# A fused attention and GEGLU block on one core: the head's loads and warm-ups, three weight tiles, and a new plan for every engine

## The chip, the cores and the metric

The kernel runs on one core of one Trainium2 chip. The time is the device time of one launch in microseconds. A core has TensorE (PE in the profile: matmuls, transposes, and its separate weight loads, PEld), VectorE (DVE), ScalarE (ACT), GpSimd (POOL) and SyncE (SP, which here only issues DMAs). They run side by side and wait for each other on semaphores. TensorE's clock is granted by a throttle; the profile shows the granted share.

Three runs of the kernel before gave 257.41, 257.42 and 258.76 us; the median is 257.42.

## The reference

One transformer block with conditioning, x being [2048, 512] in bf16:

```
mod = silu(c) @ w_mod            # six vectors of 512: sa, ca, ga, sb, cb, gb
h = layernorm(x) * (1 + ca) + sa
q, k, v = split(h @ wqkv)        # 32 heads of 16
logits[s, w] = q[s] . k[s - 2*w] / 4,  w = 0..7;  masked where s - 2*w < 0
o = softmax_w(logits) @ v[s - 2*w]
x = x + ga * (o @ wo)
h = layernorm(x) * (1 + cb) + sb
x = x + gb * ((gelu(h @ w_gate) * (h @ w_up)) @ w_down)   # inner width 1792
```

## The kernel before

**Slabs.** The 2048 rows go in four slabs of 512 (`sg` 0 to 3). Per slab: first layer norm (`norm`, VectorE statistics st and mv, rstd on GpSimd, normalised xn on VectorE), transposes to hTp in PSUM on TensorE, and their copy to hT with scale and shift (`transp_ev`, usually on ACT). Then 12 QKV groups of four 128x512 matmuls (L499), each copied out by ACT to qT, kT or vT. v goes through DRAM (`vscr`) and comes back as V4, shifted for the eight window places. VectorE multiplies q with shifted k (pq, L548, eight of 128x2048 per slab), and TensorE sums each head with 32-column matmuls (LTp, L562). ACT copies the logits to LT; they are transposed (LNp), and VectorE and ACT do the softmax (mx, LT, e, ssum, rinv). The probabilities are transposed back (PTp, PT), VectorE multiplies them with V4 (pv, L664, eight per slab), TensorE sums (o_ps, L676) and applies wo (x_ps, L696), VectorE adds x (L705). The second norm follows in the same way (LN2). The feed-forward part has 14 pairs of groups g_ps and u_ps (L724), ACT's gelu and copy (gl, ub), VectorE's product hht, and 56 matmuls y_ps with Wd (L736), an add on VectorE (ot) and a store.

**Modulation.** The six vectors are matmuls of silu(c) with blocks of w_mod (wm0 to wm5). wm1 and wm0 are wanted first (modT_ps, L324, 32 small matmuls, then ACT's copies to modT and scl, which the first hT needs), wm3 and wm4 for the second norm, wm2 and wm5 as rows (mb_ps, L338; copied to gB) by which wo and Wd are scaled on VectorE (woP L388, WdP L382).

**Tiles and queues.** wqkv is one tile of 128 x 4 x 1536, filled by three loads (one for q, one for k, one for v); the weights of a QKV group are strided columns of it. WdP takes over its buffer after the last QKV matmul. The SP queue issues, in this order: four tiles of x for slab 0, wm1, wm0, wqkv 0 and 1, x of slab 1, wqkv 2, x of slabs 2 and 3, wm2, four pieces of wo, wm3, wm4; later wm5, V4, Wg, Wu, WdP and the stores. ACT's queue only loads c. PSUM has four buffers for large results (mm), two each for the attention (att) and the transposes (tp).

**The order on each engine** is made by a small planner in the kernel's own text (`Planner`). Every stage is a generator of steps (`Op`: engine, assumed duration, what it needs, the buffers it takes and gives). At each point the planner looks for the step that can begin first, allows others on the same engine within a slack, and takes the one with the lowest due value from the table `PR` (per stage and slab). The chosen order is then fixed: each engine runs its instructions in it and only waits for semaphores. So a changed assumed duration, slack or due value reorders all engines.

**The head.** While the first loads run, TensorE runs matmuls on a zeroed tile (`warmup`, 13 at the start, and three more after modT among the transposes) so that its clock is granted. In slab 0 the four hT pieces are 512 wide, two on ACT and two on VectorE.

Of the kernel before, what the change touches and what calls it, by code (L numbers as in the profile page):

```python
# [17 lines left out]
PR = {  # L18
    "ga": 10.2, "mb": 13.7, "gb": 46.9, "wds": 31.7, "wos": 3.3, "ln1": [33, 7.6, 53.2, 33.6], "t1": [7.7,
    8.8, 0.2, 36.7], "h1": [27.6, -4.6, 27.3, 18], "qkv": [55.7, 70, 3.1, 73.3], "qev": [70, 3.6, 50, -5.6],  # L20
    "v": [23, 3, 28, 42.1], "pq": [37.5, 68.8, 111.2, 118.6], "lmm": [0, -3.1, 28.6, 13], "lev": [-13.2,
    -11.4, -3.6, 23], "smm": [7.6, 1, 66.9, 56.1], "soft": [49.9, 29.5, -6.6, 41.2], "e": [60, 20.5, -1.9,
    5.6], "ptp": [-1.9, 37.5, 19.8, 2.5], "pt": [-7.8, 1.3, 60.8, 29.5], "pv": [-4.8, 27.7, 27, 77.3], "pvmm":
    [-3.9, -0.4, 5, 23.9], "pvev": [2.3, 34.7, 76.2, -4.9], "x1mm": [-4.5, 28.3, 3, 16.2], "x1": [8, 0, 40,
    3], "ln2": [21, -5.2, -2, 3], "t2": [24.9, 1.2, -1.7, 28], "h2": [-21.4, 15.2, 3.9, 73.9], "ffn": [78.2,
    36.9, 67.9, 132.2], "act": [20.9, 46.5, -1.1, 30.2], "hh": [8, 25.1, 77.1, 8], "st": [8.2, 85, 3.8, 28.2],
# [25 lines left out]
class Planner:  # L52
# [5 lines left out]
    def __init__(self):  # L58
        self.clock = {e: 0.0 for e in self.LAT}
        self.threads = []  # L60
        self.done = {}
        self.slack = {"PE": 0.31, "ACT": 13.31, "DVE": 0, "POOL": 0, "SP": 0}
        self.far = {"PE": 0, "ACT": 0.03, "DVE": 0.2, "POOL": 0, "SP": 0}
        self.table = None
        self.quad = False
        self.dma = 0.0
        self.log = []
# [19 lines left out]
    def run(self):  # L87
# [5 lines left out]
        while live:  # L93
# [18 lines left out]
            if eng == "PE":  # L112
                if self.quad and not op.quad:
                    w += 0.1
                self.quad = op.quad
# [23 lines left out]
def kernel(  # L139
# [26 lines left out]
    def pool(name, bufs, **kw):  # L166
# [5 lines left out]
          "wm": 1, "hh": 16, "o": 2, "wA": 1, "mm": 4, "att": 2, "tp": 2}  # L172
# [28 lines left out]
    wqkv = pools["wA"].tile([P, DT, 3 * D], BF16, name="wqkv", tag="wA")  # L201
# [39 lines left out]
    def warmup(n, zero):  # L241
        if zero:
            yield Op("DVE", 0.25, lambda: nc.vector.memset(gB[:], 0.0), fire="warm")
        for k in range(n):
            def f(k=k):
                if k == 0:
                    B["warm"] = T("mm", [P, SG], F32, "warm_ps")
                nc.tensor.matmul(B["warm"][:], lhsT=gB[:, 0:P], rhs=gB[:], start=True, stop=True)
            yield Op("PE", 0.43, f, after=["warm"] if zero else ["warm", "mp0"], take=[SL["mm"]] if k == 0 else [],
                     give=[SL["mm"]] if k == n - 1 else [])  # L250
# [3 lines left out]
    def loads():  # L254
# [3 lines left out]
        def ldx(sg, c0=0, c1=CPS):  # L258
            def f():
                if c0 == 0:  # L260
                    B["x", sg] = T("x", [P, CPS, D], BF16, "x")
                nc.sync.dma_start(out=B["x", sg][:, c0:c1, :],  # L262
# [3 lines left out]
        def ldwm(b):  # L266
            def f():
                B["wm", b] = T(WM[b], [P, 4, D], BF16, "wm")
                nc.sync.dma_start(
# [11 lines left out]
        def ldq(b):  # L281
            return ld(wqkv[:, :, b * D:(b + 1) * D], wq_v[:, :, b * D:(b + 1) * D])

        def ldwd():
            B["WdP"] = T("wA", [P, FT, D], BF16, "WdP")
            nc.sync.dma_start(out=B["WdP"][:], in_=B_w_down.rearrange("(ft p) d -> p ft d", p=P))
# [5 lines left out]
        def act_q():  # L292
            yield Op("ACT", 0.55, ldc, fire="c", lat=0.05, dma=True)

        def sp_q():
            for k in range(CPS):
                yield Op("SP", 0.5, ldx(0, k, k + 1), fire=f"x0.{k}", lat=mb(0.125))
            yield Op("SP", 0.55, ldwm(1), take=[SL[WM[1]]], fire="wm1", lat=mb(0.5))
            yield Op("SP", 0.55, ldwm(0), take=[SL[WM[0]]], fire="wm0", lat=mb(0.5))
# [14 lines left out]
            yield Op("SP", 0.65, ldwd, fire="Wd", lat=mb(1.8), take=[SL["wA"]], after=[f"qkv.{g}.l" for g in range(NSG)])  # L314
# [31 lines left out]
    def mods():  # L346
# [4 lines left out]
        def f1():  # L351
            B["scp"] = T("tp", [P, 2, SG], BF16, "scp")
            nc.tensor.transpose(B["scp"][:, 0, 0:4], s4[:], ident[0:4, 0:4])
        yield Op("PE", 0.2, f1, after=["s4", "ident"], take=[SL["tp"]], fire="scp")

        def f2():
            nc.scalar.copy(out=scT[:], in_=B["scp"][:, 0, 0:4])
        yield Op("ACT", 0.2, f2, after=["scp"], give=[SL["tp"]], fire="scT")

        yield Op("PE", 0.6, cols(1, 1, "mp0"), after=["wm1", "scT"], take=[SL["mm"]], give=[SL["h2"]])  # L360
        yield Op("PE", 0.6, cols(0, 0, "mp0"), after=["wm0"], give=[SL["h2"]], fire="mp0")
# [7 lines left out]
    def mods_b():  # L369
        yield Op("PE", 0.6, cols(3, 0, "mp1"), after=["wm3", "scT", "wm4"], take=[SL["mm"]], give=[SL["h2"]])  # L370
        yield Op("PE", 0.6, cols(4, 1, "mp1"), after=["wm4"], give=[SL["h2"]], fire="mp1")
# [7 lines left out]
    def wdscale():  # L379
        for h in range(7):  # L380
            def wds(h=h):
                nc.vector.tensor_tensor(out=B["WdP"][:, 2 * h:2 * h + 2, :], in0=B["WdP"][:, 2 * h:2 * h + 2, :],  # L382
                                        in1=_ap(gB[:], [[0, 2], [1, D]]), op=ALU.mult)
            yield Op("DVE", 0.63, wds, after=["gb", "Wd"], fire=f"WdS{h}")
# [11 lines left out]
    def norm(key, src, ready, ev, parts=((0, 4),)):  # L396
# [8 lines left out]
        for c4 in range(CPS):  # L405
# [5 lines left out]
            yield Op("DVE", 0.80, f, after=ready(c4), fire=f"{ev}.st{c4}")  # L411
            for a, b in parts:
                if c4 == b - 1:
                    def f(a=a, b=b):
                        nc.vector.tensor_scalar_add(out=st_k["rstd"][:, a:b], in0=st_k["mv"][:, a:b, 1], scalar1=1e-5)  # L415
                    yield Op("DVE", 0.15, f, fire=f"{ev}.ve{a}")
# [4 lines left out]
                    yield Op("POOL", 1.1, f, after=[f"{ev}.ve{a}"], fire=f"{ev}.rs{a}")  # L421
# [10 lines left out]
    def transp(key, ev):  # L432
        for dtp in range(2):
# [7 lines left out]
            yield Op("PE", 0.52, f, after=[f"{ev}.x3", "ident"], take=[SL["tp"]], give=[SL["xn"]] if dtp else [],  # L441
                     fire=f"{ev}.t{dtp}")

    def transp0(key, ev):
        for half in range(2):
# [9 lines left out]
            yield Op("PE", 0.52, f, after=[f"{ev}.x{2 * half + 1}", "ident"], take=[] if half else [SL["tp"]] * 2,  # L455
# [4 lines left out]
    def transp_ev(key, dkey, dtag, sc, bi, ev, dep, dve_share):  # L460
        for dtp in range(2):
            for dd in range(2):
                dt = 2 * dtp + dd

                def f(dt=dt, dtp=dtp, dd=dd):
                    if dt == 0:
                        B[dkey] = T(dtag, [P, DT, SG], BF16, dtag)
                    hp = B[key, dtp]
                    if dve_share and dd == 1:
                        nc.vector.tensor_scalar(out=B[dkey][:, dt, :], in0=hp[:, dd, :], scalar1=sc(dt), scalar2=bi(dt),  # L470
                                                op0=ALU.mult, op1=ALU.add)
                    else:
                        nc.scalar.activation(out=B[dkey][:, dt, :], in_=hp[:, dd, :], func=ACT.Identity,
                                             scale=sc(dt), bias=bi(dt))
                onv = dve_share and dd == 1
                yield Op("DVE" if onv else "ACT", 0.54 if onv else 0.68, f, after=[f"{ev}.t{dtp}"] + dep,
                         take=[SL[dtag]] if dt == 0 else [], give=[SL["tp"]] if dd == 1 else [], fire=f"{ev}.h{dt}")
# [9 lines left out]
    def ln1_ev(sg):  # L487
        yield from transp_ev(("xn1", sg), ("hT", sg), "hT", lambda d: scl[:, d:d + 1], lambda d: modT[:, d:d + 1],
                             f"LN1.{sg}", ["mod0"], sg == 0)

    QKV = [(0, 0), (1, 0), (2, 0), (2, 1), (2, 2), (2, 3), (0, 1), (1, 1), (0, 2), (1, 2), (0, 3), (1, 3)]

    def qkv(sg):
        for n, (blk, j) in enumerate(QKV):
# [335 lines left out]
```

## Time and profile before

| what | value |
|---|---|
| median of three runs | 257.42 us |
| span of the profiled execution, first to last instruction | 256.4 us (no time of its own is given for it beside the span) |
| TensorE busy | 247.3 us, 96% |
| VectorE busy | 185.1 us, 72% |
| ScalarE busy | 142.3 us, 55% |
| mean granted TensorE clock | 0.979 |
| chain that ended last: TensorE | 89% of the span |
| first g_ps of the feed-forward part | 79.39 us |
| end of the last y_ps matmul on the chain | 252.9 us; the last add and the last store follow |
| read from memory, written | 21.32 MB, 4.19 MB |

A group's row gives the engine, the result and the operands, the number of instructions, the busy time and the mean of one. A wait's row gives the instruction that waited, the one that the profile takes to have released it, and the time. A row of the table by stretches has from and to, the length, then per engine the busy time and the number of instructions, and at the end the granted clock, the DMA engines' share and GB/s. The releaser is inferred, and of several semaphores the one that came last by the profile is named.

### The profile page before, as it was taken

What the parts mean: (1) busy time and instruction counts of PE and PEld (TensorE: products, weight loads), DVE (VectorE), ACT (ScalarE), POOL (GpSimd) and SP (SyncE); (2) the same over time, 40 slices, a digit from 0 to 9 for tenths busy, and PEclk for the clock granted to TensorE, in tenths of its full rate; (3) what the DMA queues carried; (4) which work ended last, traced back from release to release, by engine and by line L of the source; (5) the groups of instructions that cost most, each with busy time, mean ns of one, the idle gap of its engine ahead of it and who ended that gap; (6) DMA issues with size and microseconds to landing.
All of it is one profiled execution on the core that took longest, in us unless ns stands there. A gap on an engine that the chain in (4) does not pass through costs nothing.

```text
span 256.4 us, 3821 instructions
## 1 busy us (share of the span) xinstructions
PE 247.3 (96%) x1465; PEld 113.6 (44%) x1465; DVE 185.1 (72%) x298; ACT 142.3 (55%) x237; POOL 14.9 (6%) x39
## 2 busy tenths in 40 slices
PE   8769999999999999999999999999999999999994
PEld 2425545543464443445443345544344544444441
DVE  5459899999999999899999994577949322222121
ACT  2216786997369867522877637606754810666400
POOL 4410202000010000001000001000001000000000
PEclk9759999999999999999999999999999999999999
DMA  6999798951995300970100591010000001000011
GB/s 174 355 327 254 201 197 177 368 209 36 197 219 182 105 3 5 209 119 23 41 20 4 116 197 22 16 45 22 3 0 1 3 20 42 20 4 0 0 41 41
DMA packets 22858, 25.76 MB, mean 100 GB/s; under 512 B 952, under 2 KB 21688, under 8 KB 22840
## 3 DMA queue, kind: packets, MB, share of 16 engines
q1 hardware_dynamic: 22832, 25.52, 38.9%
q8 instruction: 11, 0.18, 0.3%
q14 instruction: 7, 0.06, 0.1%
q10 hardware_dynamic: 8, 0.00, 0.0%
HBM read 21.32 MB, written 4.19 MB: 99 GB/s over the span
## 4 chain that ended last, share of the span: by engine, by line
PE 89%; DVE 5%; DMA 3%; SPq 1%; issue 0%; DVEq 0%
PE g_ps L724 19%; PE u_ps L724 19%; PE y_ps L736 19%; PE qkv_ps L499 15%; PE x_ps L696 5%; DMA x<-in_A_x_dram 3%; PE o_ps L676 3%; PE LTp L562 3%; PE hTp L440 2%; DVE st L409 1%; PE LNp L594 1%; DVE pq L548 1%; PE PTp L646 1%; PE mb_ps L338 1%; SPq L262 1%; DVE LT L612 1%
## 5 line engine op out<-in xcount | busy, mean ns | idle before, releaser
L724 PE MATMUL g_ps<-h,Wg 128*128 128x512 bf16 x224 | 57.6, 380 | 0.0
L724 PE MATMUL u_ps<-h,Wu 128*128 128x512 bf16 x224 | 57.5, 379 | 0.0
L747 ACT ACTIVATE gl<-g_ps 128x512 bf16<-128x512 f32 x56 | 33.7, 601 | 32.0 <-PE g_ps L724 31.8
L499 PE MATMUL qkv_ps<-hT,wqkv 128*128 128x512 bf16 x192 | 47.7, 397 | 2.6 <-DVE st L409 2.6
L736 PE MATMUL y_ps<-WdP,hht 128*128 128x512 bf16 x224 | 50.0, 379 | 0.0
L765 DVE TENSOR_TENSOR hht<-gl,ub 128x512 bf16<-128x512 bf16 x56 | 23.1, 418 | 31.3 <-ACT ub L754 31.3
L754 ACT CAST ub<-u_ps 128x512 bf16<-128x512 f32 x56 | 33.0, 589 | 15.2 <-PE u_ps L724 15.2
L548 DVE TENSOR_TENSOR pq<-qT,kT 128x2048 bf16<-128x2048 bf16 x32 | 37.7, 1218 | 2.0 <-ACT kT L515 2.0
L664 DVE TENSOR_TENSOR pv<-PT,V 128x2048 bf16<-128x2048 bf16 x32 | 37.7, 1217 | 0.8 <-ACT PT L652 0.8
L736 PEld LDWEIGHTS <-hht 128*128 128x128 bf16 x224 | 21.7, 98 | 26.4 <-issue 0.8
L724 PEld LDWEIGHTS <-Wg 128*128 128x128 bf16 x224 | 20.9, 98 | 28.0 <-issue 4.9
L724 PEld LDWEIGHTS <-Wu 128*128 128x128 bf16 x224 | 21.3, 98 | 26.4 <-issue 2.1
L499 PEld LDWEIGHTS <-wqkv 128*128 128x128 bf16 x192 | 21.1, 117 | 25.4 <-issue 10.4
L772 DVE TENSOR_TENSOR ot<-y_ps,x 128x512 bf16<-128x512 f32 x16 | 11.0, 685 | 20.8 <-PE y_ps L736 20.8
L409 DVE BATCH_NORM_STATS2 st<-x 128x6 f32<-128x512 bf16 x32 | 21.8, 680 | 2.7 <-DMA x<-in_A_x_dram 2.3
L419 POOL TENSOR_TENSOR rstd<-rstd,neghalf 128x4 f32<-128x4 f32 (+1 forms) x9 | 10.4, 1155 | 181.9 <-DVE rstd L415 181.9
L696 PE MATMUL x_ps<-woP,oT 128*128 128x512 bf16 x64 | 15.8, 379 | 0.0
L513 ACT CAST qT<-qkv_ps 128x512 bf16<-128x512 f32 x16 | 9.5, 596 | 9.1 <-PE qkv_ps L499 9.1
L426 DVE TENSOR_SCALAR xn<-x,mv,rstd 128x512 bf16<-128x512 bf16 x32 | 11.4, 406 | 1.4 <-POOL rstd L419 1.4
L705 DVE TENSOR_TENSOR x<-x_ps,x 128x512 bf16<-128x512 f32 x16 | 10.8, 676 | 2.0 <-PE x_ps L696 2.0
L515 ACT CAST kT<-qkv_ps 128x512 bf16<-128x512 f32 x16 | 9.6, 598 | 4.8 <-PE qkv_ps L499 4.8
L519 ACT CAST vT<-qkv_ps 128x512 bf16<-128x512 f32 x16 | 9.4, 593 | 4.6 <-PE qkv_ps L499 4.6
(66 smaller groups left out, 179.7 us busy)
## 6 DMA issues: line engine op xcount, KB each, us to landing
V<-vscr SPq DMA_DIRECT2D x12, 520.0 KB, 7.7
wm<-in_w_mod_dram SPq DMA_DIRECT2D x6, 512.0 KB, 7.4
vscr<-vT SPq DMA_DIRECT2D x4, 512.0 KB, 3.9
out_dram<-ot SPq DMA_DIRECT2D x16, 128.0 KB, 1.7
Wg<-in_B_w_gate_dram SPq DMA_DIRECT2D x1, 1792.0 KB, 9.7
Wu<-in_B_w_up_dram SPq DMA_DIRECT2D x1, 1792.0 KB, 13.5
WdP<-in_B_w_down_dram SPq DMA_DIRECT2D x1, 1792.0 KB, 7.6
wqkv<-in_A_wqkv_dram SPq DMA_DIRECT2D x3, 512.0 KB, 8.0
```

The source lines that it names most:

```text
L409: nc.vector.bn_stats(out=st_k["st"][:, c4, :], in_=src()[:, c4, :])
L426: nc.vector.tensor_scalar(out=B[key][:, c4, :], in0=src()[:, c4, :], scalar1=st_k["mv"][:, c4, 0:1], scalar2=st_k["rstd"][:, c4:c4 + 1], o ...
L499: nc.tensor.matmul(ps[:], lhsT=wqkv[:, dt, blk * D + j:(blk + 1) * D:4], rhs=B["hT", sg][:, dt, :], start=(dt == 0), stop=(dt == DT - 1))
L548: nc.vector.tensor_tensor(out=pq[:], in0=_ap(B["qT", sg][:, j, :], [[0, 4], [1, SG]]), in1=_ap(kT[:, j, k0:k0 + SG], [[2, 4], [1, SG]]), o ...
L664: nc.vector.tensor_tensor(out=t[:], in0=_ap(B["PT", sg][:, wg, :], [[0, 4], [1, SG]]), in1=B["V4", sg][:, :, j, c0:c0 + SG], op=ALU.mult)
L696: nc.tensor.matmul(ps[:], lhsT=B["oT", sg][:, j, c4 * P:(c4 + 1) * P], rhs=woP[:, j, :], start=(j == 0), stop=(j == 3))
L724: nc.tensor.matmul(ps[:], lhsT=Wt[:, dt, ft * P:(ft + 1) * P], rhs=B["h2T", sg][:, dt, :], start=(dt == 0), stop=(dt == DT - 1))
L736: nc.tensor.matmul(ps[:], lhsT=B["hh", sg, ft][:, c4 * P:(c4 + 1) * P], rhs=B["WdP"][:, ft, :], start=(ft == 0), stop=(ft == FT - 1))
L747: nc.scalar.activation(out=gl[:], in_=B["g", sg, ft][:], func=ACT.Gelu_apprx_tanh)
L754: nc.scalar.copy(out=ub[:], in_=B["u", sg, ft][:])
L765: nc.vector.tensor_tensor(out=hh[:], in0=B["gl", sg, ft][:], in1=B["ub", sg, ft][:], op=ALU.mult)
L772: nc.vector.tensor_tensor(out=ot[:], in0=B["y", sg, c4][:], in1=B["x", sg][:, c4, :], op=ALU.add)
```

## The change

1. `wqkv` becomes three tiles of 128 x 4 x 512, one per load. Wd becomes four tiles with four loads: three take over the buffers of the weight tiles, the fourth (half as large) has its own.
2. Two of slab 0's x tiles and wm0 are loaded from ACT's queue; SP issues the other two, wm1, and then the rest in the old order.
3. In slab 0 the copy to hT is done in pieces of 256 columns per half of the rows, four on ACT and four on VectorE (`transp0_ev`).
4. `warmup` has 19 matmuls in one thread of low urgency (60), which the planner puts where TensorE has nothing else: ten, then s4's transpose, two, modT of wm1, two, modT of wm0, five, then all 16 transposes of slab 0.
5. Slab 0 computes q and k of the first two column sets before v (`QKV0`).
6. The small transpose of silu(c) goes into an att buffer instead of a tp buffer.
7. Every due value, the slacks and several assumed durations are new, and the planner charges both changes between 32-column and full matmuls. All engines' orders differ: modT of wm3 and wm4 and mb_ps of wm2 come before slab 1's QKV, woP's scaling after slab 3's statistics, wm5's load between slab 0's V loads, and the 32-column matmuls are visited in 27 places instead of 30.

```
-    wqkv = pools["wA"].tile([P, DT, 3 * D], BF16, name="wqkv", tag="wA")
+    wqkv = [pools["wA"].tile([P, DT, D], BF16, name=f"wqkv{b}", tag="wA") for b in range(3)]
+    Wd3 = wts.tile([P, 2, D], BF16, name="Wd3")
...
-            yield Op("PE", 0.43, f, after=["warm"] if zero else ["warm", "mp0"], take=[SL["mm"]] if k == 0 else [],
+            yield Op("PE", 0.427 if k < cold else 0.216, f, after=["warm"], take=[SL["mm"]] if k == 0 else [],
...
         def act_q():
-            yield Op("ACT", 0.55, ldc, fire="c", lat=0.05, dma=True)
+            yield Op("ACT", 0.46, ldc, fire="c", lat=0.0, dma=True)
+            for k in (1, 3):
+                yield Op("ACT", 0.46, ldx(0, k, k + 1, nc.scalar), fire=f"x0.{k}", lat=mb(0.125), dma=True)
+            yield Op("ACT", 0.46, ldwm(0, nc.scalar), take=[SL[WM[0]]], fire="wm0", lat=mb(0.5), dma=True)
         def sp_q():
-            for k in range(CPS):
-                yield Op("SP", 0.5, ldx(0, k, k + 1), fire=f"x0.{k}", lat=mb(0.125))
-            yield Op("SP", 0.55, ldwm(1), take=[SL[WM[1]]], fire="wm1", lat=mb(0.5))
-            yield Op("SP", 0.55, ldwm(0), take=[SL[WM[0]]], fire="wm0", lat=mb(0.5))
+            for k in (0, 2):
+                yield Op("SP", 0.47, ldx(0, k, k + 1), fire=f"x0.{k}", lat=mb(0.125 if k else 0.0))
+            yield Op("SP", 0.47, ldwm(1), take=[SL[WM[1]]], fire="wm1", lat=mb(0.5))
...
-            yield Op("SP", 0.65, ldwd, fire="Wd", lat=mb(1.8), take=[SL["wA"]], after=[f"qkv.{g}.l" for g in range(NSG)])
+            for b in range(4):
+                yield Op("SP", 0.65, ldwd(b), fire=f"Wd{b}", lat=mb(0.5 if b < 3 else 0.25), take=[SL["wA"]] if b < 3 else [],
+                         after=[f"qp.{NSG - 1}.{blk}.3" for blk in range(3)])
...
+    def transp0_ev(key, dkey, sc, bi, ev, dep, onv):
+        for half in range(2):
+            for dt in (1, 3) if onv else (0, 2):
+                def f(dt=dt, half=half):
+                    if dkey not in B:
+                        B[dkey] = T("hT", [P, DT, SG], BF16, "hT")
+                    o, i = B[dkey][:, dt, half * 256:half * 256 + 256], B[key, dt // 2][:, dt % 2, half * 256:half * 256 + 256]
+                    if onv:
+                        nc.vector.tensor_scalar(out=o, in0=i, scalar1=sc(dt), scalar2=bi(dt), op0=ALU.mult, op1=ALU.add)
                     else:
+                        nc.scalar.activation(out=o, in_=i, func=ACT.Identity, scale=sc(dt), bias=bi(dt))
...
+    QKV0 = [(0, 0), (1, 0), (0, 1), (1, 1), (2, 0), (2, 1), (2, 2), (2, 3), (0, 2), (1, 2), (0, 3), (1, 3)]
...
-                    nc.tensor.matmul(ps[:], lhsT=wqkv[:, dt, blk * D + j:(blk + 1) * D:4], rhs=B["hT", sg][:, dt, :],
+                    nc.tensor.matmul(ps[:], lhsT=wqkv[blk][:, dt, j::4], rhs=B["hT", sg][:, dt, :],
...
-    pl.spawn(0.5, warmup(13, True))
-    pl.spawn(30, warmup(3, False))
+    pl.spawn(60, warmup(13, 19))
```

Besides these lines the diff holds the new `PR` table, the slacks, the assumed durations, and the users of the new tiles.

## The prediction

> **What bounds the kernel now.** I read the page first, then the table by stretches, the waits and the chain. The page says TensorE:
>
> ```profile
> PE 247.3 (96%) x1465; PEld 113.6 (44%) x1465; DVE 185.1 (72%) x298; ACT 142.3 (55%) x237; POOL 14.9 (6%) x39
> ...
> PEclk9759999999999999999999999999999999999999
> ```
>
> The only loose time on TensorE is in slices 1 to 3, where its clock is low too. The table by stretches shows it: nothing in 12.82 to 15.18, then five us at half clock, then TensorE full in nearly every stretch (200 to 240 us shown for all).
>
> ```profile
> 12.82:15.18 2.36, 0.00 (x1) 0.03 (x1) 1.74 (x5) 0.00 (x0) 0.00 (x0) 0.50 1.10 348
> 15.18:20.20 5.02, 5.02 (x12) 1.77 (x13) 2.92 (x7) 1.30 (x3) 1.03 (x1) 0.50 1.10 295
> 20.20:25.00 4.80, 4.80 (x31) 2.76 (x30) 4.62 (x15) 3.21 (x6) 0.00 (x0) 0.99 0.94 252
> 200.00:240.00 40.00, 40.00 (x199) 18.64 (x198) 9.45 (x21) 20.76 (x36) 0.00 (x0) 1.00 0.04 14
> ```
>
> So the time is: when the QKV stream starts, plus half-clock time, plus a full TensorE. What holds the start? The waits name a statistics instruction for the 2.6 us, but that had no business there. The timeline and the DMA list tell more:
>
> ```profile
> PE qkv_ps L499 <- DVE st L409: 2.6, 1, 2.6
> DVE hT L470 <- ACT hT L473: 3.2, 1, 3.2
> DVE pq L548 <- ACT kT L515: 2.0, 1, 2.0
> DVE woP L388 <- ACT gB L343: 1.1, 1, 1.1
> ```
>
> ```profile
> 11.95 0.63 PE L499 MATMUL qkv_ps<-hT,wqkv 128*128 128x512 bf16 x1
> 15.18 9.38 PE L499 MATMUL qkv_ps<-hT,wqkv 128*128 128x512 bf16 x31 [2.59 <-DVE st L409]
> ```
>
> ```profile
> wqkv<-in_A_wqkv_dram SPq DMA_DIRECT2D x1, 512.0 KB, 9.2
> ```
>
> One QKV matmul runs at 11.95, the next at 15.18. The third weight load was issued at 5.82 and took 9.2 us: 15.02. The build's waits agree: the second weight load of the array waits for all three loads of the one tile, since its strided columns span the others' columns. The hT tile was ready at 13.0 (VectorE's second piece). The other rows are VectorE's idle time before the first FFN; it is otherwise full there (29.43 of 30 us in 35 to 65), so it could be next.
>
> From the chain, the price of a visit to the 32-column matmuls:
>
> ```profile
> 82.15 0.55 PE LTp L562 x8
> 82.69 0.97 PE u_ps L724 x4
> 83.66 0.86 PE g_ps L724 x4
> ```
>
> Eight cost 0.55 and 0.11 on the next group; two eights together 0.98 + 0.11. Per visit 0.23 is overhead.
>
> **The change, part by part.** The profiled span is 256.4; the median 257.42 lies 1.0 above it, which I keep as the time around the span.
>
> *Three weight tiles.* The first QKV group then needs only load 0 (landed 10.5), the second load 1 (12.2), the fifth load 2 (15.0, four groups of 0.865 later). The 2.2 us from 13.0 to 15.2 are gone; hT is late next.
>
> *Loads from two queues.* ACT issues two x tiles and wm0, SP is relieved of three issues (0.43, 0.43, 0.49). wm0 landed at 9.04. Best case it gains the whole 1.35, worst nothing: the DMA engines are full from 5.5 us on. I take 7.9, x1 at 12.8 instead of 13.56, since between 3 and 5.5 us the DMA share was 0.55 to 0.93 and can be filled. The Trainium skill (DMA: Bandwidth & Descriptors, Issuing engines are not separate DMA queues) says that two issuing engines share the same DMA engines and save only issue time; by it no load gains more than that. ACT's table load moves from 1.4 to about 2.8 behind its issues; s4 is ready at about 4.4, and the PE reaches it after ten warm-ups at 5.6, so this is free.
>
> *Scaling per half.* VectorE had to wait for ACT's piece of the same PSUM tile (the 3.2 us row), and the changed build keeps such waits: ACT's first piece waits for the 12th of 16 transposes, then the pieces alternate ACT, VectorE, VectorE, ACT. A 256-wide piece isn't in the trace: on ACT it is between 0.16 (4 wide) and 0.72 (pitch at 512), on VectorE between 0.16 and 0.54; halfway, 0.45 and 0.36. The first matmul waits for five pieces in a row: 0.48 + 0.36 + 0.36 + 0.48 + 0.48 and latencies, about 2.4 (bounds 1 and 3.3). So the halves win little.
>
> *Warm-up.* On TensorE the order is now ten, s4's transpose, two, modT, two, modT, five, then 16 transposes. Behind wm0: modT 0.5, five at 0.216 (1.1; 2.1 at half clock), 12 transposes 0.7 (1.3), latency 0.1. QKV starts at 7.9 + 2.4 + 2.4 = 12.7. That is 2.5 earlier.
>
> *The clock.* Before lost half of 15.18 to 20.33, 2.6 us. After: ends 0 and 3.0 (half rate to 20.3 from a start of 14.4). The nearest row is the clock's fall at 10.08: the 3.41 us window before it had TensorE busy 1.9 us. The new head has a gap of some 2.4 us between transposes and QKV, so a window with as little work is likely; I take one half-rate window, 1.7.
>
> *VectorE up to the first FFN.* Both orders hold the same work from x1's statistics to LN2.0's last xn (16 pq, 8 pv, 16 statistics, one softmax and a third): 13.56 to 75.3. It starts 0.75 earlier, the 2.0 for kT goes (kT is there at about 15.5, pq at 16.2) and the 1.1 for woP (its scaling is put 10 instructions later). ACT now has a q copy between the two pairs of h pieces: +0.6. So VectorE allows the first g_ps at 79.4 - 3.2 = 76.2, or 75.6 if its small gaps (0.6) close. TensorE allows it at 12.7 + (79.4 - 15.2 - 2.6 - 0.2) + 1.7 = 75.8. The two are level, and with each waiting a little for the other (the mask waits for a late LTp copy) I take 76.3: 3.1 earlier.
>
> *Behind it.* Quad visits fall from 30 to 27, all three after the first g_ps: -0.7. Walking the two orders through FFN 0, o_ps waits for pv 3, 4 and 7, 8 some 0.25 and 0.2: +0.4, bounds 0 and 2 since VectorE has hardly idle time to 150 us. wm5's load waits on SP for mb2, with the last V piece queued behind it: that is needed at about 48 us and issued by 29, so free. Wd as four loads costs SP three issues of about 0.5 and starts with the last QKV reads (about 73); its first scaling is at about 82, 8 us later, against 7.6 to landing. The tail (56 y_ps, last add, store) is the same.
>
> Sum: -3.1 - 0.7 + 0.4 = -3.4 on a span of 256.4 gives 253.0, and 254.0 as a time.
>
> **The rivals.**
>
> *The clock stays full.* If a clock once up falls only when TensorE does nothing for a whole window, a gap of 2.4 us costs nothing: TensorE could start the FFN at 74.1, but VectorE holds it at about 75.8; 0.5 better, 253.5. For it: warm-ups now stand in the waits for wm1 and wm0. Against: the window before the fall at 10.08 was not idle. The Trainium skill has this as its rule (TensorE: Matmul & The Clock Gate, What's actually happening: the clock falls after an idle window); the trace is harsher, and with the rule the clock's term would be 0 instead of 1.7.
>
> *The clock never rises in the head.* The first unbroken run is 12 warm-ups and a small transpose, about 5.2 us from 1.25, where before had 13 at 5.6. A 3.41 us window fits in it only in some positions, and the window 10.08 to 13.49, 73% busy, did not raise it. Then QKV starts at 7.9 + 0.5 + 2.1 + 1.3 + 0.2 + 2.4 = 14.4 and loses 3.0: 17.4 against 15.2 + 2.6 = 17.8. With -0.7 + 0.4 that is 256.7, within 0.5% (1.3 us, about what a measurement of this kernel can tell from no change).
>
> *Slower: the second norm's modulation blocks.* modT of wm3 and wm4 now stands on TensorE before slab 1's QKV, and its copy on ACT before the last pieces of hT for slabs 1 and 2; pq and LTp wait behind. Both need wm4, which landed at 25.6 (issued 16.2, 9.4 to landing); TensorE comes there at about 25. Each us later is lost: the gain of 3.4 is gone at 29, slower by over 0.5% from 30.3; at 32 it is 260.4. Against it: wm4 goes out no later than before, and the V loads stand behind it.
>
> *More than the sum.* If wm0 and x1 gain all 1.35 and the gaps close: TensorE's bound with a full clock, 12.2 + 61.4 = 73.6, then -5.8 - 0.7 = 250.9.
>
> **How the numbers follow.** The sum's case has 0.42, at 254.0 (own range 253.2 to 255.0); the full clock 0.20 at 253.5; more 0.06 at 251 to 252.5; stalls of the replanned orders up to the bound of 2 us 0.10, at 255 to 256; the clock that never rises 0.14 at 256.7; slower 0.08 at 259 to 262. Range 252.3 to 257.0, which leaves out the slower case and half of "more". Faster 0.77, same 0.15, slower 0.08.
>
> **What would show it.** Right: no wait of QKV on a load, the second matmul directly behind the first; start at 12 to 13.5; granted clock half in at most one window after it; VectorE's first pq without idle time; first g_ps at 75.5 to 77. Wrong: modT with idle time near 25 us; a half clock to 20 us; TensorE idle for over 1 us at LTp, o_ps or y_ps after 30 us.

## The result and the profile after

The changed kernel is slower, by about 1%. Twenty runs have a median of 260.39 us (256.89 to 264.11) beside 257.97 (256.69 to 259.22) for twenty of the kernel before, 0.9% more. The ratio is 1.0061, 95% interval 1.0034 to 1.0088; it leaves out the runs that are over 1.5% above the fastest of the same kernel, here seven of the changed kernel's (260.94 and above). A second, smaller set (e11_after_again, below) gave 260.70 beside 257.67, ratio 1.0138 (1.0100 to 1.0176). The forecast was 254.0. The time of one kernel moves by several microseconds from run to run, in part with the mean granted clock (the changed kernel: 256.89 us at 0.993, 258.2 to 261.6 at 0.978 to 0.987, 261.1 to 264.1 at 0.966 to 0.974), so below I use medians, and read single traces for places and waits. The sets of runs were taken on several chips, each with runs of the kernel before beside it (medians 257.49 to 258.12); ratios are always to those.

The profiled execution took 260.13 us, with a span of 258.0 (before: 256.4). Its page, busy time by engine and the clock in 40 slices:

```profile
PE 247.3 (96%) x1468; PEld 114.4 (44%) x1468; DVE 184.7 (72%) x300; ACT 144.2 (56%) x239; POOL 14.5 (6%) x39
...
PEclk9878999999999999999999999999999999999999
```

TensorE is busy for the same 247.3 us as before; the loss is idle time, and the clock dips in slices 2 and 3. The timeline of TensorE over the head and at the one later gap (start, length, instructions, and in brackets idle time with what ended it):

```profile
10.20 0.56 PE L337 MATMUL modT_ps<-scT,wm 128*128 128x1 bf16 x16 [2.53 <-DMA wm<-in_w_mod_dram]
10.62 2.29 PE L251 MATMUL warm_ps<-gB 128*128 128x512 bf16 x5
12.71 1.67 PE L466 MATMUL hTp<-ident,xn 128*128 128x128 bf16 x16
16.69 12.36 PE L526 MATMUL qkv_ps<-hT,wqkv 128*128 128x512 bf16 x48 [2.32 <-ACT hT L496]
...
43.81 1.04 PE L351 MATMUL mb_ps<-wm,scB 128*128 128x512 bf16 x4 [0.88 <-DMA wm<-in_w_mod_dram]
```

Read it as a chain. wm0 is late (2.53 us of idle time), then modT, then five warm-up matmuls that nobody needs but that stand in order, then the transposes, then 2.32 us for the scaled pieces, and only then QKV: 16.69 instead of 15.18, and instead of the 12.7 of the forecast. From there on QKV runs without a gap; it no longer waits for a weight load. The chain that ended last has both loads of `wm` in it (start, length):

```profile
2.25 7.90 DMA wm<-in_w_mod_dram
...
32.29 11.47 DMA wm<-in_w_mod_dram
43.81 1.04 PE mb_ps L351 x4
```

The first is wm0 on ACT's queue. The second is wm5, whose load stands on SP behind three V loads: 11.47 us, where before it was issued at 26.34 and took 3.5. The SP queue, after (two lines) and before:

```profile
29.61 1.94 SPq L561 DMA_DIRECT2D V<-vscr  x3
32.29 0.38 SPq L274 DMA_DIRECT2D wm<-in_w_mod_dram  x1
...
26.34 0.37 SPq L269 DMA_DIRECT2D wm<-in_w_mod_dram  x1
```

The table by stretches, cut within some 0.15 us of where the clock changes (length, then busy time of PE, PEld, DVE, ACT, POOL; then granted clock, DMA share, GB/s):

```profile
10.41:13.83 3.42, 3.42 (x30) 2.04 (x27) 0.00 (x0) 0.24 (x2) 0.28 (x1) 0.52 1.10 349
13.83:17.24 3.41, 1.09 (x10) 0.67 (x8) 2.06 (x5) 2.15 (x4) 0.00 (x0) 0.98 1.10 349
17.24:20.65 3.41, 3.41 (x10) 1.26 (x9) 2.63 (x8) 1.17 (x2) 0.47 (x1) 0.52 1.08 241
20.65:25.00 4.35, 4.35 (x21) 2.22 (x20) 4.21 (x9) 2.58 (x5) 0.56 (x1) 0.98 0.67 202
200.00:240.00 40.00, 40.00 (x199) 18.59 (x197) 9.87 (x22) 20.68 (x36) 0.00 (x0) 1.00 0.04 14
```

Two stretches of half clock, one over the five warm-ups and the transposes, one over the first QKV matmuls (1.7 us lost there). Between them TensorE worked 1.09 of 3.41 us at full clock. The waits of ScalarE and VectorE:

```profile
DVE hT L494 <- ACT hT L496: 6.1, 2, 5.8
ACT hT L496 <- PE hTp L466: 3.2, 1, 3.2
```

VectorE stands still for 5.8 us before its first hT piece, and x1's statistics stand behind those pieces in its order, though x1 had landed at 12.7: they start at 16.54, 3 us later than before. The first g_ps starts at 81.84 (before 79.39), and from there to the last group of y_ps it is 160.60 us (before 161.25). So the loss lies wholly ahead of the first FFN, 2.45 us: 1.51 in the head, 0.88 at wm5 and 0.30 at the last LTp ahead of the FFN (0.45 us of waiting for VectorE, before 0.15). Another 0.2 is one QKV matmul that the kernel before had already run at 11.95. Half clock behind QKV's start costs 0.9 less than before (1.7 for 2.6); that leaves some 0.5 that I have not separated.

### The profile page after: what moved, and what is told of

The parts are those of the page before. It is cut to its first block, busy times and chain, and to the rows that moved or that the text cites. A ratio compares the mean times of both kernels' runs of the same rounds, so it can differ in the third digit from the quotient of the medians.

```text
span 258.0 us, 3834 instructions
## 1 busy us (share of the span) xinstructions
PE 247.3 (96%) x1468; PEld 114.4 (44%) x1468; DVE 184.7 (72%) x300; ACT 144.2 (56%) x239; POOL 14.5 (6%) x39
## 4 chain that ended last, share of the span: by engine, by line
PE 87%; DMA 8%; DVE 3%; ACT 1%; ACTq 1%; issue 0%; DVEq 0%
PE g_ps L751 19%; PE u_ps L751 19%; PE y_ps L763 19%; PE qkv_ps L526 13%; DMA wm<-in_w_mod_dram 8%; PE x_ps L723 5%; PE o_ps L703 3%; PE LTp L589 3%; PE hTp L453 2%; DVE pq L575 1%; PE LNp L621 1%; PE warm_ps L251 1%; PE mb_ps L351 1%; PE PTp L673 1%; ACT hT L496 1%; DVE LT L639 1%
## 5 line engine op out<-in xcount | busy, mean ns | idle before, releaser
L763 PE MATMUL y_ps<-Wd,hht 128*128 128x512 bf16 x224 | 49.8, 379 | 0.0
L526 PE MATMUL qkv_ps<-hT,wqkv 128*128 128x512 bf16 x192 | 46.8, 391 | 2.3 <-ACT hT L496 2.3
L774 ACT ACTIVATE gl<-g_ps 128x512 bf16<-128x512 f32 x56 | 33.7, 601 | 17.9 <-PE g_ps L751 16.6
L432 POOL TENSOR_TENSOR rstd<-rstd,neghalf 128x4 f32<-128x4 f32 (+1 forms) x9 | 9.7, 1077 | 182.8 <-DVE rstd L428 182.8
L481 ACT ACTIVATE h<-hTp,modT,scl 128x512 bf16<-128x512 bf16 x16 | 11.5, 782 | 6.7 <-PE hTp L453 6.7
L713 ACT CAST oT<-o_ps 128x512 bf16<-128x512 f32 x16 | 9.3, 587 | 6.9 <-PE o_ps L703 6.9
## 6 DMA issues: line engine op xcount, KB each, us to landing
Wu<-in_B_w_up_dram SPq DMA_DIRECT2D x1, 1792.0 KB, 13.4
```

Of the source, the lines that this page charges most:

```text
L481: nc.scalar.activation(out=B[dkey][:, dt, :], in_=B[key, dtp][:, dd, :], func=ACT.Identity, scale=sc(dt), bias=bi(dt))
L526: nc.tensor.matmul(ps[:], lhsT=wqkv[blk][:, dt, j::4], rhs=B["hT", sg][:, dt, :], start=(dt == 0), stop=(dt == DT - 1))
L763: nc.tensor.matmul(ps[:], lhsT=B["hh", sg, ft][:, c4 * P:(c4 + 1) * P], rhs=B["Wd", ft // 4][:, ft % 4, :], start=(ft == 0), stop=(ft == F ...
L774: nc.scalar.activation(out=gl[:], in_=B["g", sg, ft][:], func=ACT.Gelu_apprx_tanh)
```

## The experiments

The theory tested is S, a series: wm0's landing, modT, five warm-ups, transposes, pieces; TensorE is the bound from QKV on, so each microsecond of the head and each wait is one of the time. The first expectations call it A. Against it: the new orders after the head set the time (R), VectorE does (V), or the warm-ups earn their time through the clock (W).

**wm0 on SP, directly behind wm1 (e1_wm0_sp).**

```diff
-            yield Op("ACT", 0.46, ldwm(0, nc.scalar), take=[SL[WM[0]]], fire="wm0", lat=mb(0.5), dma=True)
+            yield Op("ACT", 0.46, lambda: None, take=[SL[WM[0]]], fire="wm0", lat=mb(0.5), dma=True)
...
-            yield Op("SP", 0.47, ldwm(1), take=[SL[WM[1]]], fire="wm1", lat=mb(0.5))
+            def wm10():
+                ldwm(1)()
+                ldwm(0)()
+            yield Op("SP", 0.47, wm10, take=[SL[WM[1]]], fire="wm1", lat=mb(0.5))
```

> The changed kernel with one edit: wm0 is issued by SP directly behind wm1 instead of by ACT; every engine's order is else the same. Theory A (the head's chain: wm0's landing, modT, five warm-ups, transposes and the alternating hT pieces stand in series before QKV): wm0 lands at about 8.1 instead of 10.15, QKV starts at about 14.6 instead of 16.7, and the time falls from 260.4 to about 258.5. Rival R (the new orders set the time, the head is absorbed): wm0 lands earlier, but the time stays above 259.7.

Measured: median 258.16 (255.88 to 259.54), ratio to before 1.0019 (0.9989 to 1.0048), 2.2 below the changed kernel's median (1.9, when each is taken against the kernel before of its own set). QKV started at 14.67, 2.0 earlier; the line of the chain that shows why:

```profile
2.18 6.20 DMA wm<-in_w_mod_dram
```

Issued at the same time as on ACT's queue, wm0 landed at 8.38 instead of 10.15. In the changed kernel wqkv0, issued on SP at 2.19, landed at 9.4, ahead of wm0: the two queues shared the DMA engines, which were full (in the changed kernel a DMA share of 1.09 from 6.41 to 10.00), and the load that the head needs first came second. e1 shows that wm0's place in SP's order brings the time back. That ACT's queue is in itself served later than SP's is not ruled out: wm0 on ACT with wqkv0 put behind it was not run.

**The last five warm-ups left out (e2_no_five).**

```diff
-                nc.tensor.matmul(B["warm"][:], lhsT=gB[:, 0:P], rhs=gB[:], start=True, stop=True)
+                if k < 14:
+                    nc.tensor.matmul(B["warm"][:], lhsT=gB[:, 0:P], rhs=gB[:], start=True, stop=True)
```

> The changed kernel without the last five warm-up matmuls (between modT of wm0 and the transposes; they compute nothing that is used). Theory A: QKV starts 1.1 us earlier at full clock and 2.2 us earlier at half clock, at about 14.5, and the time falls to about 258.3. Rival R: above 259.7. Rival W (the five are needed for the clock): the clock stays half for a window more and eats the gain, the time is above 259.7 with a lower granted clock.

Measured: 258.69 (257.59 to 260.46), ratio 1.0040 (1.0013 to 1.0067); QKV at 14.71, also 2.0 earlier. The profiled run had half clock from 9.76 to 19.92 without a break, and still the time fell by 1.7 (1.3 against the kernel before of each set). W had the longer half clock right (three windows of 3.4 us in place of two), but not the time: the five cost more in line than they earn. The intervals of this ratio and of the changed kernel's 1.0061 overlap, so the size rests on the run with the five moved, below.

**Both (e3_both).** The two diffs above together.

> Both edits together: wm0 from SP and no five warm-ups. Theory A: QKV starts at about 12.5, the time is about 256.4, below the kernel before. Rival R: above 259.5.

Measured: QKV at 11.71, 5.0 us ahead of the changed kernel, and yet a median of 260.10 (255.98 to 260.58). The six runs are too scattered for a ratio: 255.98 and 258.33, and four from 259.95 to 260.58. The traced one is that of 258.33, 1.8 below the changed kernel's traced 260.13: the time did not follow the start by 5.0. TensorE's timeline says where the start was lost again:

```profile
36.92 1.03 PE L530 MATMUL qkv_ps<-hT,wqkv 128*128 128x512 bf16 x4
40.54 1.89 PE L355 MATMUL mb_ps<-wm,scB 128*128 128x512 bf16 x4 [2.60 <-DMA wm<-in_w_mod_dram]
42.22 4.32 PE L530 MATMUL qkv_ps<-hT,wqkv 128*128 128x512 bf16 x16
```

The wait for wm5 grew from 0.88 to 2.60, and half clock followed from 40.2 to 43.6: mb_ps took 1.89 instead of 1.04, the next sixteen 4.32 instead of 3.62. The first g_ps came at 80.08, only 1.8 earlier. The wait for wm5 was 0.9, 1.7, 1.0 and 2.6 us in the changed kernel, e1, e2 and e3, where TensorE came to mb_ps at 42.9, 40.9, 41.7 and 37.9: longer, the earlier it came. It is not the arrival alone, since the landing moves too: a second trace of the changed kernel (e11_after_again) came at 42.45 and waited 1.52. It is a new wait that takes back part of any gain in the head. This is R in a narrow form: not all the orders, one place in SP's. The four longer runs have no trace, so whether they lost more at the same place is not shown.

**Three weight tiles alone (e4_before_tiles).** The kernel before, with the tiles and their loads and users from the change; no instruction's order moves.

```diff
-    wqkv = pools["wA"].tile([P, DT, 3 * D], BF16, name="wqkv", tag="wA")
+    wqkv = [pools["wA"].tile([P, DT, D], BF16, name=f"wqkv{b}", tag="wA") for b in range(3)]
+    Wd3 = wts.tile([P, 2, D], BF16, name="Wd3")
```

> The kernel before with the weights as three tiles and Wd as four (four loads issued one behind the other where the one was), and nothing else: its orders are unchanged. Theory A: QKV runs on at 13.0 instead of 15.2 and pq 0 comes about 2 us earlier; the time falls by about 2.0 to 256.0. Rival: VectorE or the third weight load (15.0, wanted by the third group) holds the rest and less than 0.7 is gained.

Measured: 256.39 (255.12 to 257.52), ratio 0.9948 (0.9921 to 0.9975): faster than both kernels. The timeline:

```profile
11.29 0.38 PE L503 MATMUL qkv_ps<-hT,wqkv 128*128 128x512 bf16 x1 [0.28 <-ACT hT L477]
11.87 1.91 PE L503 MATMUL qkv_ps<-hT,wqkv 128*128 128x512 bf16 x7 [0.20 <-DVE hT L474]
14.92 5.37 PE L503 MATMUL qkv_ps<-hT,wqkv 128*128 128x512 bf16 x24 [1.14 <-DMA wqkv<-in_A_wqkv_dram]
```

The wait for all three loads is gone and the third load costs 1.14 at v's first block. The median is 0.4 short of the 256.0 expected; in this trace TensorE also waits 0.63, 0.29 and 0.71 us for modulation loads between 23 and 29 us, where the kernel before did not wait. Whatever made the change slower, it is not this part.

**wm5 ahead of the V loads (e5_wm5), and with both head edits (e6_head_wm5).** The V loads of slab 0 are put off until wm5 is issued, as in the kernel before:

```diff
-            yield Op("SP", 0.65, ldwm(5), take=[SL[WM[5]]], fire="wm5", lat=mb(0.5))
+            def wm5():
+                ldwm(5)()
+                for g in vlate:
+                    g()
+            yield Op("SP", 0.65, wm5, take=[SL[WM[5]]], fire="wm5", lat=mb(0.5))
...
-            yield Op("SP", 0.65, f, after=[f"vst.{sg}", "M2"],
+            yield Op("SP", 0.65, (lambda f=f: vlate.append(f)) if sg == 0 and w4 < 3 else f, after=[f"vst.{sg}", "M2"],
```

> The changed kernel with one edit: the load of the sixth modulation block (wm5) stands ahead of slab 0's V loads on SP, as in the kernel before, instead of behind three of them. Nothing else in any engine's order moves. The changed kernel showed the load 11.47 us from issue to landing and 0.88 us of TensorE idle at its mb_ps. Theory S (the stages stand in series, TensorE is the bound from the first QKV matmul on): the wait goes, the first g_ps stands at 81.0 instead of 81.9, the time is 0.9 lower than the changed kernel's, 259.5 by its median of 260.4. Rival V (VectorE's order sets when the first g_ps can begin): the wait goes and the first g_ps stays at 81.5 to 81.9, the logit products wait that much longer, the time is 260.4.

Measured: 258.94 (256.62 to 259.96), ratio 1.0043 (1.0010 to 1.0076). No wait of mb_ps is left. The first g_ps stood at 81.70, but in this run half clock lasted to 22.24, and QKV's first 48 matmuls took 13.20 instead of 12.36; less that 0.84 it is 80.9, as S had it. The gain in time lies inside the intervals, so by itself this run decides little.

> The wm5 load moved as in the run before, on top of the two head edits of e3_both (wm0 issued by SP behind wm1; the last five warm-ups left out). e3_both began QKV at 11.71, then lost 2.60 us waiting for wm5 at 37.9 and 1.6 us to a stretch of half clock at 40.2 to 43.6 right behind that wait; its first g_ps stood at 80.1. Theory S: both losses go, the first g_ps stands at 75.9, span 252.2, time 254.3. Rival V: the logit products wait for VectorE instead, the first g_ps stands at 77.2 to 78, time 255.6 to 256.4. Rival C (the clock's window at 40 us is not due to the wait): the wait goes alone, first g_ps 77.5, with half clock shown somewhere in 20 to 60 us.

Measured: 254.28 (253.06 to 256.56), ratio 0.9872 (0.9830 to 0.9914). QKV at 12.47, no wait at mb_ps, no half clock near 40 us, first g_ps 76.56:

```profile
12.47 12.37 PE L534 MATMUL qkv_ps<-hT,wqkv 128*128 128x512 bf16 x48 [2.31 <-ACT hT L504]
...
38.54 1.03 PE L359 MATMUL mb_ps<-wm,scB 128*128 128x512 bf16 x4
...
76.23 0.40 PE L599 MATMUL LTp<-pq,Mph 128*32 128x512 bf16 x4 [0.45 <-DVE pq L585]
```

S had 254.3; that the median meets it to 0.02 is luck, since the profiled run (254.82) started QKV 0.76 later than e3_both and the first g_ps 0.66 later than S's 75.9, and one window of half clock stands in its head (13.4 to 16.9). The last line is also the answer to V: TensorE waits for VectorE's products 0.45 us ahead of the FFN, the same 0.45 as in the changed kernel at 81.5. It is 0.45 in every trace with the new orders, whether the first g_ps stands at 75.16 (e9_fill) or at 84.47 (e10_five_behind, where a load held TensorE for 4.29 us): VectorE comes earlier and later with TensorE, so it is not what held it. With three local edits the changed kernel goes from 1.0061 (or 1.0138) of the kernel before to 0.9872.

**Whole pieces (e7_whole).** e6_head_wm5 with the scaling in four pieces of 512 columns.

```diff
-                    o, i = B[dkey][:, dt, half * 256:half * 256 + 256], B[key, dt // 2][:, dt % 2, half * 256:half * 256 + 256]
+                    if half != (dt > 1):
+                        return
+                    o, i = B[dkey][:, dt, :], B[key, dt // 2][:, dt % 2, :]
```

> e6_head_wm5 with one more edit: the first layer norm's transposes are scaled in four whole pieces of 512 columns, as in the kernel before, instead of eight of 256. In e3_both the half pieces took 0.56 us (ScalarE) and 0.40 (VectorE), and QKV began 2.31 us behind the last transpose; in e4_before_tiles the whole ones took 0.77 and 0.54, and QKV's first matmul began 0.71 behind it, its second 1.29. Theory S: QKV's first matmul at 10.2 and without gaps from 10.8, 1.1 us ahead of e6_head_wm5's, first g_ps and time 1.1 lower than e6_head_wm5's. Rival V: QKV earlier by the same, first g_ps and time as in e6_head_wm5, since VectorE's x1 statistics wait for their load at 12.4 either way.

Measured: 254.09 (253.00 to 254.83), ratio 0.9859 (0.9830 to 0.9888), the same as e6_head_wm5. Half clock lay over 9.36 to 16.08 in this run and over 13.44 to 16.8 in that one, so the sizes can't be compared; inconclusive.

**q and k first (e8_q_first).** e4_before_tiles with `QKV0` for slab 0.

```diff
+    QKV0 = [(0, 0), (1, 0), (0, 1), (1, 1), (2, 0), (2, 1), (2, 2), (2, 3), (0, 2), (1, 2), (0, 3), (1, 3)]
-        for n, (blk, j) in enumerate(QKV):
+        for n, (blk, j) in enumerate(QKV if sg else QKV0):
```

> e4_before_tiles (the kernel before with three weight tiles) with the changed kernel's order of slab 0's first blocks: q0 k0 q1 k1 ahead of the four v blocks. e4_before_tiles waited 1.14 us for the third weight load behind q0 k0. Theory S: the wait goes, the first g_ps stands at 76.1 instead of 77.2, the time is 1.1 lower, 255.3. Rival V: the logit products or mb_ps wait longer by what is gained, first g_ps 77.2, time 256.4.

Measured: 255.69 (255.17 to 256.46), ratio 0.9923 (0.9897 to 0.9949). The wait for the third load is gone and the first g_ps stands at 76.42. S's size was 1.1; the medians give 0.7, and the two intervals overlap. The trace does not give the gain to the new order:

```profile
10.51 0.38 PE L505 MATMUL qkv_ps<-hT,wqkv 128*128 128x512 bf16 x1 [0.28 <-ACT hT L477]
18.65 1.70 PE L444 MATMUL hTp<-ident,xn 128*128 128x128 bf16 x16 [0.47 <-DVE xn L430]
```

In this run QKV began 0.78 us earlier than in e4_before_tiles (10.51 for 11.29; its modulation loads kept TensorE waiting less), and the first g_ps came 0.74 earlier. From QKV's start to the first g_ps it is 65.91 us, in e4_before_tiles 65.87. The 1.14 us went into a new wait for VectorE's xn: 0.47 ahead of slab 1's transposes, and 0.64 more while they ran (1.70 us for 1.06). So V holds here in another place than it named, as far as one trace of each tells.

**Filling the gap behind the transposes (e9_fill, and once more as e13_halves_fill).** e6_head_wm5 with seven matmuls there:

```diff
+                if half:
+                    fill = T("mm", [P, SG], F32, "fill_ps")
+                    for _ in range(7):
+                        nc.tensor.matmul(fill[:], lhsT=gB[:, 0:P], rhs=gB[:], start=True, stop=True)
```

> e6_head_wm5 with seven dependence-free matmuls of 128x512 placed behind the sixteen transposes, in the 2.31 us in which TensorE waited for the scaled pieces; at full clock they take 7 x 0.216 = 1.5 us. In e6_head_wm5 the clock fell to half from 13.4 to 16.8 us, one window behind that gap, which cost half of 3.36 us, 1.7 us. Theory C1 (a window of the clock with long idle stretches of TensorE sends the next to half): the window goes in most runs, QKV still begins near 12.5, median 252.8 to 253.3. Theory C2 (the fall at the start does not depend on filling this gap): half clock in the first 20 us as before, median 254.3. Rival Q (the matmuls are in the way): QKV begins up to 0.8 later, median 255.

> e9_fill once more on the same chip: 253.5, QKV 2.3 us behind the last transpose.

Measured: 253.50 (253.03 to 254.19), ratio 0.9859 (0.9820 to 0.9899), then 253.35 (253.10 to 255.23), 0.9837 (0.9797 to 0.9877). The first profile shows full clock through the head, over stretches in which the kernels above fell to half:

```profile
9.54 1.46 PE L479 MATMUL fill_ps<-gB 128*128 128x512 bf16 x6
11.80 10.68 PE L538 MATMUL qkv_ps<-hT,wqkv 128*128 128x512 bf16 x47 [0.81 <-ACT hT L508]
```

```profile
10.00:13.50 3.50, 2.69 (x13) 1.20 (x12) 2.38 (x7) 2.06 (x4) 0.53 (x2) 1.00 1.10 348
13.50:17.00 3.50, 3.50 (x18) 1.86 (x17) 3.36 (x8) 2.39 (x5) 0.85 (x1) 1.00 1.10 349
```

QKV is not later for it (2.3 us behind the last transpose, as without), so Q falls. (One of the seven matmuls and one of QKV's 48 have no record in this trace.) The second profile of the same kernel still has half clock from 10.3 to 13.7, behind waits of 1.17 and 0.48 us for the modulation loads. In the four traces with filling behind the transposes (e9_fill, e13_halves_fill, and e10 and e12 below) no new fall follows that gap; so C1 holds for this gap, not for the head. It is not worth much here: two of e6_head_wm5's six runs have a mean granted clock of 1.000 without any filling, the 0.8 to 0.9 us by medians is inside the intervals, and 253.50 just misses C1's 252.8 to 253.3.

**The five moved behind the transposes (e10_five_behind).** The changed kernel; its own last five warm-ups, in that gap.

```diff
+                if k < 14:
+                    nc.tensor.matmul(B["warm"][:], lhsT=gB[:, 0:P], rhs=gB[:], start=True, stop=True)
...
+                    fill = T("mm", [P, SG], F32, "fill_ps")
+                    for _ in range(5):
+                        nc.tensor.matmul(fill[:], lhsT=gB[:, 0:P], rhs=gB[:], start=True, stop=True)
```

> The changed kernel with its last five warm-up matmuls behind the sixteen transposes, in the gap before QKV, instead of ahead of them; nothing else moves. In the changed kernel they took 2.1 to 2.3 us of the chain in front of QKV (10.62 to 12.71). Theory S: QKV begins at 14.7 as in e2_no_five, 2.0 us ahead of the changed kernel's 16.7, time 2.0 lower than it, 258.4 by 260.4. Theory C1 adds: half clock ends earlier than in e2_no_five (9.8 to 19.9), 1.7 us less lost, time 256.7. Rival R (what starts earlier is lost again at the wait for wm5): mb_ps waits 1.7 to 2.0 us, time 259.

> The changed kernel as it is, beside the two runs above on one chip: 260.4, ratio to the kernel before 1.006.

Measured on one chip: 257.89 (256.49 to 262.75) for the moved five, ratio 1.0006 (0.9973 to 1.0039), beside 260.70, 1.0138 (1.0100 to 1.0176), for the changed kernel as it is. The intervals are apart: where the five stand costs about 1.3% by the ratios, 1.1% by the medians. S's 258.4 and C1's 256.7 lie on either side of it. The upper end, 262.75, is the profiled run. QKV began at 14.93 in it, and half clock in the head ended at 15.1, not at 19.9 as in e2_no_five; both are as forecast. But it shows the wait of e3_both at its worst, longer than R's 1.7 to 2.0, with half clock behind it from 42.4 to 49.2:

```profile
43.77 1.89 PE L352 MATMUL mb_ps<-wm,scB 128*128 128x512 bf16 x4 [4.29 <-DMA wm<-in_w_mod_dram]
```

**Whole pieces again, at full clock (e12_whole_fill).** e9_fill with the diff of e7_whole and two filling matmuls instead of seven.

> e9_fill with the scaling in four whole pieces of 512 columns instead of eight of 256, and two matmuls of filling behind the transposes instead of seven. e7_whole against e6_head_wm5 told nothing, since half clock stood at different places of the two. In e9_fill the transposes ended at 9.48 and QKV began at 11.80 and ran without a gap. Theory H (eight pieces that alternate between ScalarE and VectorE on one bank cost more than four): QKV's first matmul 0.7 behind the last transpose, its block done 1.0 to 1.2 sooner than in e9_fill counted from the last transpose, time 252.5 against 253.5. Rival K (matmuls of the first block wait for later pieces, so that the block ends no sooner): the block ends 2.8 to 3.2 behind the last transpose in both, time 253.5. Rival C1 (the shorter filling lets the clock fall): half clock at 10 to 17 us, time 254 to 255.

Measured: 253.58 (253.10 to 253.69), ratio 0.9828 (0.9794 to 0.9861) beside 253.35 for the halves on the same chip: no difference. ScalarE's timeline, with full clock throughout:

```profile
9.36 0.78 ACT L510 ACTIVATE hT<-hTp,modT,scl 128x512 bf16<-128x512 bf16 x1 [0.52 <-PE hTp L474]
11.20 0.78 ACT L510 ACTIVATE hT<-hTp,modT,scl 128x512 bf16<-128x512 bf16 x1 [1.06 <-DVE hT L508]
```

QKV's first matmul came at 10.19, 0.7 behind the transposes, but it ran without gaps only from 12.03; two matmuls having gone before, the block is 0.2 ahead of e9_fill's. So K holds, not H: in this order ScalarE's second piece waits for both of VectorE's, and four pieces one after another last as long as eight. In e4_before_tiles ScalarE's two stand next to each other (10.46 to 11.9), VectorE's beside the second (11.27 to 12.5), and the block runs from 11.87. I read from it that the order between the engines counts more than the size of the pieces; a run that changes the order alone was not made.

## Why the prediction was wrong, point by point

- *Three weight tiles: right.* QKV waits for no weight load, and the tiles alone gain 0.5% (e4).
- *Loads from two queues: the step "I take 7.9" failed.* I let wm0 gain 1.1 us because the DMA share between 3 and 5.5 us left room. It landed at 10.15, 1.1 later than before (9.04): on ACT's queue it stood beside wqkv0 on SP instead of ahead of it, and ahead of it again, in e1, it landed at 8.38. My bounds, a gain of 1.35 or nothing, held no loss. e1 prices it at 2.0 us of QKV's start and 1.9 to 2.2 of the time. x1 was right (12.7 for 12.8). The forecast had told that the DMA engines are full from 5.5 us on, and did not ask whose packets fill them. The Trainium skill (DMA: Bandwidth & Descriptors, Issuing engines are not separate DMA queues) says that transfers from two issuing engines run on the same DMA engines and interleave; the trace agrees, and the sequel is what I missed: whatever interleaves loses its place in the order.
- *Warm-up: the place was right, the price half.* "Five at 0.216 (1.1; 2.1 at half clock)" took 2.1, since the clock had fallen at about 10.5, behind the 2.53 us wait for the late wm0. e2 prices it at 2.0 us of the start, e2 and e10 at 1.7 to 2.8 of the time. With wm0 2.25 late, the warm-ups 1.0 and the transposes 0.6 longer, the start of 12.7 becomes 16.6; measured 16.69.
- *Scaling per half: right.* 2.5 us from the end of the twelfth transpose (14.16) to QKV, forecast 2.4. One piece took 0.56 us on ScalarE and 0.41 on VectorE, more than the 0.45 and 0.36 put halfway between two rows. "So the halves win little" is what e12 shows.
- *The clock: one stretch in QKV was right (1.7), another was over the warm-ups.* The rival of the clock that stays full falls, and so does the one of the clock that never rises: full clock came back at 13.9 us, ahead of QKV. The rule of the first, from the Trainium skill (TensorE: Matmul & The Clock Gate, What's actually happening), is a fall after an idle window of some 3.4 us; here the clock fell behind 3.41 us with 1.09 us of work, so the trace is harsher, as the forecast had said.
- *VectorE up to the first FFN: the cap was not reached.* x1's statistics began at 16.54, not 12.8, since I had not put them behind the late hT pieces. The wait of LTp for VectorE was 0.45 us all the same. Of TensorE's 6.0 us between the forecast of 75.8 for the first g_ps and the measured 81.84, 4.0 lie in the head, 0.9 at wm5 and 0.45 here; 0.7 remains, 0.2 of it the one QKV matmul named above.
- *Behind it: the step "so free" failed.* I looked at the V load queued behind wm5, and not at wm5 queued behind three V loads. It was issued at 32.29 and not by 29, took 11.47 us to land, and mb_ps waited 0.88 (1.52 in e11_after_again). This alone is small. But it is the wait that comes next whenever the head gets faster: 2.60 us, and 1.6 more of half clock, in e3. Had the head run as forecast, the sum would have failed here.
- *Fewer visits: right; the stalls beside them: wrong.* -0.7 forecast for three visits fewer; from the first g_ps to the last y_ps group it is -0.65. The +0.4 for o_ps behind pv did not show: TensorE has no idle time there in either kernel.
- *Around the span: 1.0 was wrong.* I took one run's span and the median of others. Each run since, of every kernel here, has 2.0 to 2.1 us between span and time; the forecast span of 253.0 would have been a time of 255.0.
- *"More than the sum": 12.2 does not follow from its own terms.* With wm0 at 9.04 - 1.35 = 7.7 the start is 12.5, and the time 251.2. Nothing else rests on it.

The slower rival had 259 to 262, and the measured time lies in it, but by luck: modT of wm3 and wm4 at 30.43 waited for nothing. What made the kernel slower was a load one place too far back in the head and five matmuls one place too far forward; what kept the repair from paying was a third load.

The fastest version is e9_fill (253.5 and 253.35 in two sets, 0.9859 and 0.9837 of the kernel before), with e12_whole_fill no different from it: the change with wm0 on SP behind wm1, wm5 ahead of the V loads, and seven matmuls behind the transposes in place of the last five warm-ups. How much of it belongs to the new tables of orders and how much to the tiles was not separated; e8, the tiles and `QKV0` with the old orders, reaches 0.9923 (0.9897 to 0.9949).

## What to carry to other kernels

A load that is moved to a second queue is no longer ahead of what it was ahead of: ask which loads it now shares the engines with, and bound the landing from the late side too. Work that only keeps a clock up belongs in a gap that is there anyway, behind the work that others wait for; ahead of it, it is a stage of the chain, and at half clock it costs double. When a start is made earlier, look for the next load that the engine will meet sooner: a wait of 0.9 us that seemed too small to matter grew to 2.6, and with the half clock behind it took back 3.2 us of a start made 5.0 us earlier.

## What the runs showed of the hardware that I had not expected

- The half-clock stretches are 3.4 us or a multiple of it (3.42, 3.41, 3.36 in these traces; 6.7 in e7_whole and 10.2 in e2_no_five, where they follow each other, 13.6 in e5_wm5), and where they fall differs between runs of one kernel: the same kernel ran its head at full clock in e9_fill and had one such stretch in e13_halves_fill.
- A pause far from the head can bring the clock down: 2.60 us without work at 38 us brought 3.4 us of half clock (e3_both), 4.29 us at 39.5 brought 6.8 (e10_five_behind). Shorter pauses at the same place, 0.88 to 1.66 us in the changed kernel, e1, e2 and e11, brought none. The share of busy time alone does not decide it: counted in steps of 3.41 us from the nearest change of the clock, TensorE was busy for 1.9 us ahead of the fall at 10.08 in the kernel before, and for 1.75 us from 39.90 to 43.31 in e1_wm0_sp, where no fall followed.
- Two loads of 512 KB issued 0.06 us apart on two queues, with other loads ahead of them, landed 0.75 us apart, the one on SP's queue first (9.4 against 10.15), though SP's queue held more loads. One pair of one trace; what decides it was not tried.
